# Sliding-window attention with a channel mix: batch 5's q and k through the DMA crossbar, batch 0's tail tokens in another row order

## The chip, the cores and the metric

The kernel runs on one core of one Trainium2 chip. The metric is the device time of one execution in microseconds (us), as the median of several runs. TensorE (PE) does matmuls and transposes, ScalarE (ACT) and VectorE (DVE) work on tiles elementwise, GpSimd (POOL) and SyncE (SP) issue most of the DMA transfers. Each engine executes its own list of instructions in order, and semaphores tie the lists together.

## The reference

Attention with a causal window of 128 tokens and a linear distance bias per head, followed by an RWKV channel mix over the concatenated heads:

```python
def _attn_ref(q, k, v):                 # [8 batches, 8 heads, 576 tokens, 64]
    ...
    scores = scale * np.matmul(q, k.transpose(0, 1, 3, 2))
    ...
    bias = slopes[:, None, None] * (-np.abs(rel).astype(np.float32))[None, :, :]
    mask = (rel >= 0) & (rel < window)
    ...
    return np.matmul(attn, v).astype(np.float32)      # attn: softmax of the masked scores

def _moe_ref(x, mu_k, mu_r, w_k, w_v, w_r):           # x: [8, 576, 512]
    ...
    xk = mu_k * x + (1.0 - mu_k) * x_prev             # x_prev: x one token earlier
    xr = mu_r * x + (1.0 - mu_r) * x_prev
    k = np.maximum(xk @ w_k, 0.0)                     # 512 to 1024
    v = k * k @ w_v                                   # 1024 to 512
    r = 1.0 / (1.0 + np.exp(-(xr @ w_r)))
    return (r * v).astype(np.float32)
```

Inputs and output are float32; the kernel computes in bf16 with float32 sums.

## The kernel before

**Tiles.** A batch has 576 tokens: four blocks of 128 and a tail of 64. Heads go in pairs (`g`, four of them), one head in each half of the 128 partitions. For each batch and pair the kernel brings q and k into a layout with the head dimension on partitions, computes scores (`scores`, matmuls on L727 into the PSUM tiles `duo`), takes exp on ACT (L741 into `at`), multiplies by a mask of bias and window on DVE (L754), and multiplies by v (`attend`, L782), where a column of ones gives the softmax sum. DVE divides (L788, L794 into `xu`), the result is transposed into `xt`, and DVE mixes it with its shifted self into `xk` and `xr` (L881, L888). The channel mix runs on pieces of 256 to 512 tokens out of two batches: L984 (w_k, then relu on ACT, L991, and a square on DVE or ACT into `kk`), L1002 (w_r, then tanh, L1009), L1018 (w_v) and L1023 on DVE into `ot`, which SP stores (L1048).

**Getting q and k transposed.** POOL loads a batch's q and k into one of two buffers `cb`, v into one of two `vs` and `tv`, and the tail tokens of q and k into one of two `ts`. There are two ways on. In batches 1 to 5, PE transposes blocks of `cb` by matmuls with the identity (`qk_quad` on L1079 for batches 1 and 2; `qk_some` on L838 for 3 to 5, half a batch at a time: 32 matmuls), and ACT or DVE copies the result from PSUM to one of four `qk` buffers (L697). For batches in `XB`, SP issues `dma_start_transpose` from `cb` (`flip`, L536): eight transfers per batch, one for each of q and k and each block of 128 tokens, into one of two buffers `qx`, which L727 reads directly. Each of them covers all heads, so the first score of a batch needs all eight. `full_load` reads rows in another order for batches in `XB` (`h (r p) d` instead of `h (p r) d`), with the same number of transfers. The two `qx` buffers also serve as staging space for batch 0 at the start.

**Tail tokens.** From batch 4 on, SP also transposes the tail tokens (`tail_flip`, L629) from `ts` to `tt`. Batches 1 to 3 do it on PE (L913). For batch 0 (`TW`), four tokens go into one row of 256 elements, so q and k make two loads of 128 rows (L516), and PE brings them into place with 16 matmuls on L940 against a permutation of the identity, from which DVE copies to `tt`.

**Order.** A planner at the top of the file (`Plan`) builds the program from nodes with costs. For PE, ACT and DVE the order of nodes is given by the lists in `ORDER` (node numbers, which change when nodes are added or dropped); SP and POOL issue in the order in which nodes were made, subject to when the planner thinks they are ready. 90 small matmuls on `warm` (L688) fill PE at the start. POOL's loads wait until the eighth load before them has landed.

## Time and profile before

| what | value |
|---|---|
| runs, median (lowest to highest) | 231.62 us (231.43 to 231.62), 3 runs |
| the profiled execution | 231.23 us, of which the span from first to last instruction is 229.5 us |
| granted TensorE clock | 1.0 throughout |
| DMA queue of POOL (software_dynamic) | 16.26 MB in 95,984 packets |
| DMA queue of SP and ACT (hardware_dynamic) | 13.84 MB in 23,776 packets |
| DMA transposes on SP | 16 `qx<-cb` (median 3.7 us to landing), 4 `tt<-ts` (4.5 us), 8 `xt<-xu` (2.5 us) |

Busy time counts the time in which an engine executes an instruction, over the span. PE matmuls overlap in its pipeline, so a merged row of the timeline is a little longer than the distance to the next one. The page also cuts the span into 40 slices of 5.7 us and gives the busy share of each in tenths:

```
PE   7999999999999999999999999999999999999994
ACT  3569999999899979999876757986448432435501
DMA  6999999999999999999695999996152133222005
```

PE is nearly full from the second slice on; the DMA engines are full for the first 18 slices and again around the loads of the last two batches.

### The profile page before, as it was taken

What the parts mean: (1) busy time and instruction counts of PE and PEld (TensorE: products, weight loads), DVE (VectorE), ACT (ScalarE), POOL (GpSimd) and SP (SyncE); (2) the same over time, 40 slices, a digit from 0 to 9 for tenths busy, and PEclk for the clock granted to TensorE, in tenths of its full rate; (3) what the DMA queues carried; (4) which work ended last, traced back from release to release, by engine and by line L of the source; (5) the groups of instructions that cost most, each with busy time, mean ns of one, the idle gap of its engine ahead of it and who ended that gap; (6) DMA issues with size and microseconds to landing.
All of it is one profiled execution on the core that took longest, in us unless ns stands there. A gap on an engine that the chain in (4) does not pass through costs nothing.

```text
span 229.5 us, 6623 instructions
## 1 busy us (share of the span) xinstructions
PE 220.9 (96%) x2681; PEld 134.4 (59%) x2715; DVE 189.5 (83%) x423; ACT 163.4 (71%) x295; POOL 92.6 (40%) x118
## 2 busy tenths in 40 slices
PE   7999999999999999999999999999999999999994
PEld 6576756755756656555655755545675445456542
DVE  6687799899869998988788998999979979774333
ACT  3569999999899979999876757986448432435501
POOL 8666655589878961982004970700000000000000
PEclk9999999999999999999999999999999999999999
DMA  6999999999999999999695999996152133222005
GB/s 159 177 175 190 191 161 200 190 185 158 200 130 191 163 117 184 112 144 151 139 162 90 165 167 136 107 137 198 47 95 71 46 133 73 65 93 91 3 14 214
DMA packets 121534, 31.11 MB, mean 136 GB/s; under 512 B 108184, under 2 KB 117664, under 8 KB 121504
## 3 DMA queue, kind: packets, MB, share of 16 engines
q0 software_dynamic: 95984, 16.26, 98.6%
q1 hardware_dynamic: 23776, 13.84, 25.4%
q10 hardware_dynamic: 1744, 0.59, 1.0%
q8 instruction: 21, 0.34, 0.6%
q14 instruction: 9, 0.07, 0.1%
HBM read 33.56 MB, written 9.44 MB: 187 GB/s over the span
## 4 chain that ended last, share of the span: by engine, by line
PE 74%; DMA 12%; DVE 5%; POOL 3%; issue 2%; ACT 2%; DVEq 0%; POOLq 0%; ACTq 0%
PE uno L1018 24%; PE uno L984 23%; PE uno L1002 12%; PE duo L782 7%; PE duo L727 5%; DMA wk_sb<-in_moe_w_k_dram 4%; DMA cb<-in_k_dram 4%; DMA wv_sb<-in_moe_w_v_dram 4%; PE uno L838 3%; ACT at L741 1%; DVE xk L888 1%; DVE at L754 1%; DVE ot L1023 1%; POOL vs L501 1%; POOL qx L497 1%
## 5 line engine op out<-in xcount | busy, mean ns | idle before, releaser
L984 PE MATMUL uno<-xk,wk_sb 128*128 128x256 bf16 (+2 forms) x412 | 71.9, 313 | 0.4
L741 ACT ACTIVATE at<-duo 128x1024 bf16<-128x1024 f32 (+2 forms) x68 | 65.2, 987 | 7.5 <-PE duo L727 7.3
L991 ACT ACTIVATE rl<-uno 128x256 bf16<-128x256 f32 (+2 forms) x104 | 47.3, 476 | 31.7 <-PE uno L984 23.7
L1018 PE MATMUL uno<-wv_sb,kk 128*128 128x512 bf16 (+2 forms) x277 | 67.3, 373 | 1.5 <-issue 0.6
L984 PEld LDWEIGHTS <-wk_sb 128*128 128x128 bf16 x416 | 38.6, 98 | 22.8 <-issue 0.7
L501 POOL DMA_DIRECT2D vs<-in_v_dram x32 | 28.4, 898 | 39.0 <-PE duo L782 33.5
L1018 PEld LDWEIGHTS <-kk 128*128 128x128 bf16 x296 | 27.1, 98 | 27.6 <-issue 0.5
L965 DVE TENSOR_TENSOR kk<-rl 128x256 bf16<-128x256 bf16 (+2 forms) x94 | 29.8, 339 | 13.5 <-ACT rl L991 13.3
L754 DVE TENSOR_TENSOR at<-at,mask 128x1024 bf16<-128x1024 bf16 x56 | 36.9, 686 | 2.4 <-ACT at L741 2.1
L1002 PE MATMUL uno<-wr_sb,xr 128*128 128x512 bf16 x133 | 35.6, 380 | 0.8 <-DMA wr_sb<-in_moe_w_r_dram 0.3
L1009 ACT ACTIVATE rs<-uno 128x512 bf16<-128x512 f32 x36 | 21.7, 614 | 17.0 <-PE uno L1002 11.4
L1023 DVE SCALAR_TENSOR_TENSOR ot<-rs,uno 128x512 f32<-128x512 bf16 (+2 forms) x37 | 24.2, 669 | 9.5 <-PE uno L1018 6.1
L888 DVE SCALAR_TENSOR_TENSOR xk<-dl,mu_sb,xt 128x576 bf16<-128x576 bf16 (+1 forms) x32 | 24.6, 778 | 0.2
L888 DVE SCALAR_TENSOR_TENSOR xr<-dl,mu_sb,xt 128x576 bf16<-128x576 bf16 (+1 forms) x32 | 24.7, 780 | 0.0
L782 PEld LDWEIGHTS <-at 128*128 128x128 bf16 x576 | 21.3, 98 | 4.8 <-issue 0.2
L794 DVE TENSOR_TENSOR xu<-duo,rc 128x640 bf16<-128x640 f32 x28 | 22.9, 822 | 0.5
L697 ACT COPY qk<-uno 128x512 bf16<-128x512 bf16 (+1 forms) x40 | 21.0, 586 | 1.2 <-PE uno L1127 0.9
L1002 PEld LDWEIGHTS <-xr 128*128 128x128 bf16 x144 | 13.3, 98 | 14.3 <-DMA wr_sb<-in_moe_w_r_dram 0.4
L532 POOL DMA_DIRECT2D cb<-in_k_dram x20 | 17.8, 917 | 3.8 <-DMA vs<-in_v_dram 1.9
L782 PE MATMUL duo<-vs,at 128*128 128x65 bf16 x448 | 18.8, 194 | 0.1
L532 POOL DMA_DIRECT2D cb<-in_q_dram x20 | 17.7, 923 | 2.2 <-PE uno L984 1.5
L697 ACT COPY xt<-uno 128x640 bf16<-128x640 bf16 (+3 forms) x28 | 15.1, 576 | 1.9 <-PE uno L838 0.9
(82 smaller groups left out, 200.5 us busy)
## 6 DMA issues: line engine op xcount, KB each, us to landing
out_dram<-ot SPq DMA_DIRECT2D x30, 256.0 KB, 3.9
vs<-in_v_dram POOLq DMA_DIRECT2D x32, 128.0 KB, 7.2
cb<-in_q_dram POOLq DMA_DIRECT2D x20, 128.0 KB, 6.3
cb<-in_k_dram POOLq DMA_DIRECT2D x20, 128.0 KB, 6.1
out_dram<-ot SPq DMA_DIRECT2D x10, 128.0 KB, 1.8
wk_sb<-in_moe_w_k_dram POOLq DMA_DIRECT2D x2, 512.0 KB, 8.8
cb<-in_q_dram POOLq DMA_DIRECT2D x4, 256.0 KB, 9.7
cb<-in_k_dram POOLq DMA_DIRECT2D x4, 256.0 KB, 10.0
```

The costliest lines, as they stand in the source:

```text
L501: return dma(POOL, 256, issue_t(1024), lambda e: nc.gpsimd.dma_start(out=vs_buf[h.idx][:, j, :, 0:D], in_=v[b, :, 128 * j:128 * j + 128].r ...
L532: return [dma(POOL, 256, issue_t(1024), lambda e, r=r: nc.gpsimd.dma_start(out=cb_buf[h.idx][:, i, r], in_=src[:, :, r]), [g], kind="q") f ...
L697: (nc.scalar.copy if e == ACT else nc.vector.tensor_copy)(out=out, in_=in_)
L741: lambda e, ah=ah, w=w, hp=hp: nc.scalar.activation(out=ah(), in_=two(hp)[:, :, 0:w], func=AF.Exp, scale=float(scale)), (), [hp])
L754: nc.vector.tensor_tensor(out=a, in0=a, in1=m, op=ALU.mult)
L782: nc.tensor.matmul(a[:, hl, t - t0], lhsT=at[:, lo:lo + 128], rhs=vs[:, u, 2 * g + hl, :] if u < NF else tvb[:, 2 * g + hl], start=(u == u ...
L888: lambda e: nc.vector.scalar_tensor_tensor(out=buf[hk.idx][:, g, e0 + c0:e0 + c1], in0=dls(), scalar=mu[:, g:g + 1], in1=xc(1), op0=ALU.mu ...
L965: nc.vector.tensor_tensor(out=out, in0=in_, in1=in_, op=ALU.mult)
L984: nc.tensor.matmul(one(hp)[:, 0:n], lhsT=wk_sb[:, po, 128 * fo:128 * fo + 128], rhs=xk_buf[hx.idx][:, po, c0:c1], start=(po == 0), stop=(p ...
L991: a = op(ACT, act_t(n), [s], pr, lambda e, hp=hp, hr=hr: nc.scalar.activation(out=rl_buf[hr.idx][:, 0:n], in_=one(hp)[:, 0:n], func=AF.Rel ...
L1002: nc.tensor.matmul(one(hp), lhsT=xr_buf[hx.idx][:, po, 128 * c:128 * c + 128], rhs=wr_sb[:, po], start=(po == 0), stop=(po == NPO - 1))
L1018: nc.tensor.matmul(one(hv)[:, a:b], lhsT=kk_buf[hk.idx][:, fo, o:o + 128], rhs=wv_sb[:, fo, a:b], start=(fo == 0), stop=(fo == NFO - 1))
```

## The change

Three edits and new lists. Batch 5 joins the batches whose q and k go through the DMA crossbar. In batch 0's tail load the 128 rows are ordered by token group first and head second (`c h`) instead of head first (`h c`), and the permutation in the L940 matmuls follows. The lists for PE, ACT and DVE are replaced; the numbers in them shift with the nodes that batch 5 drops and adds.

```diff
 ORDER = {
     "PE": [int(x) for x in """
-49 42 74 72 39 58 56 67 51 71 43 65 53 66 60 69 57 54 52 40 45 46 48 59 68 75 41 55 73 63 76 131 61 47 44 50 70
...
+42 76 47 65 59 73 39 58 48 50 71 68 63 74 75 41 43 55 46 61 40 66 51 52 45 56 57 67 70 53 69 131 60 44 49 72 144
...
-    XB = range(6, B)
+    XB = range(5, B)
     XO = range(6, B)
...
                     out=ts_buf[h.idx].rearrange("p h d -> p (h d)")[:, 256 * i:256 * i + 256],
-                    in_=(q, k)[i][b, :, SM:S].rearrange("h (c r) d -> h c (r d)", r=4)), [g], kind="ts"))
+                    in_=(q, k)[i][b, :, SM:S].rearrange("h (c r) d -> c h (r d)", r=4)), [g], kind="ts"))
...
                         lhsT=ts_buf[hs.idx][:, n],
-                        rhs=ident.rearrange("p (g t c) -> p t g c", g=G, t=2)[:, hl],
+                        rhs=ident.rearrange("p (c g t) -> p t g c", g=G, t=2)[:, hl],
                         start=True, stop=True)
```

On SP the order around batch 5 becomes (stores are numbered from the start of the program):

```
before: ... store 8, store 9, tail transpose b5, store 10, 2 x b6, store 11, 3 x b6, store 12, 2 x b6, store 13, 1 x b6, tail transpose b6, ...
after:  ... store 8, store 9, 8 x b5, tail transpose b5, store 10, store 11, store 12, 3 x b6, store 13, 5 x b6, store 14, tail transpose b6, store 15, store 16, 1 x b7, store 17, 7 x b7, ...
```

On PE 64 matmuls on L838 with their weight loads go. POOL's list is the same as before. The file is one line shorter, so line numbers behind the lists are lower by one.

## The prediction

> **What bounds the kernel now.** I read the page's busy line and chain first, then PE's waits cut to a window, then the chain's pieces up to 45 us, then the timelines of PE, POOL and SP around batch 5. The page:

> ```profile
> span 229.5 us, 6623 instructions
> PE 220.9 (96%) x2681; PEld 134.4 (59%) x2715; DVE 189.5 (83%) x423; ACT 163.4 (71%) x295; POOL 92.6 (40%) x118
> PEclk9999999999999999999999999999999999999999
> PE 74%; DMA 12%; DVE 5%; POOL 3%; issue 2%; ACT 2%; DVEq 0%; POOLq 0%; ACTq 0%
> ```

> TensorE is busy 96% at full granted clock, and the chain lies on it for 74%; the 12% on DMA need a place. PE's waits from 38 us to 226 us are two lines in all:

> ```profile
> PE uno L1018 <- issue: 0.6, 4, 0.2
> PE uno L1018 <- DVE at L754: 0.2, 1, 0.2
> ```

> So over 188 us PE stands for 0.8 us (total, count, longest). Work taken from PE there shortens the run one for one, and a late operand there lengthens it one for one; ACT and DVE work is hidden under PE. The chain's pieces show the DMA share:

> ```profile
> 5.73 9.91 DMA wk_sb<-in_moe_w_k_dram
> 17.42 9.35 DMA cb<-in_k_dram
> 28.20 9.28 DMA wv_sb<-in_moe_w_v_dram
> 37.52 1.02 PE uno L1018 x4
> ```

> Up to 37.5 us the chain is the stream of POOL loads: the first L1018 starts 0.04 us after its weights land. Before it PE idles 0.55 us for batch 1's tail tokens and 0.30 us for wr_sb (page lines for L913 and L1002 in its waits). That 0.85 us is what an earlier load stream can give back.

> **Part 1, batch 5's transposes leave PE.** The two bursts and what follows each:

> ```profile
> 102.97 0.63 PE L838 MATMUL uno<-ident,cb 64*128 64x64 bf16 x32
> 103.76 1.67 PE L1018 MATMUL uno<-wv_sb,kk 128*128 128x512 bf16 x7 [0.16 <-issue]
> 111.61 0.63 PE L838 MATMUL uno<-ident,cb 64*128 64x64 bf16 x32
> 112.17 1.04 PE L1018 MATMUL uno<-wv_sb,kk 128*128 128x512 bf16 x3
> ```

> The chain gives each burst of 32 matmuls 0.47 us (the 0.63 includes the drain of the last one), so 2 x 0.47 = 0.94 us go. All other PE instructions keep their number and size. The new order has 105 changes between 64-row and 128-row instructions, the old one 104; a change costs about 0.10 us (L727's last starts at 105.80, L984 at 105.92, where neighbours follow at 0.03). Net: **-0.84 us**, all in the stretch without waits.

> Off the path: of the 512-element qk copies ACT loses seven (603 ns each) and DVE one (687), and ACT takes four squares from DVE (two of 423, two of 515 ns). With one 256-element copy moved from DVE to ACT (409 against 376 ns) ACT loses 7 x 0.603 - 0.38 - 1.88 = 2.0 us and DVE 0.69 + 0.41 + 2 x 0.28 + 2 x 0.35 = 2.4 us. Costed at nothing, since PE hides both; neither gets heavier.

> Added: eight 128x512 crossbar transposes on SP, behind the ninth output store and ahead of batch 5's tail transpose and the tenth store. SP's rows:

> ```profile
> 84.50 2.99 SPq L1048 DMA_DIRECT2D out_dram<-ot  x2
> 92.38 1.22 SPq L629 DMA_TRANSPOSE tt<-ts  x1
> 105.55 0.34 SPq L1048 DMA_DIRECT2D out_dram<-ot  x1
> 105.98 3.04 SPq L536 DMA_TRANSPOSE qx<-cb  x2
> 139.59 11.94 SPq L536 DMA_TRANSPOSE qx<-cb  x8
> ```

> SP is free from 87.5 to 105.55 us but for one transpose. Batch 5's q and k land from 83.5 to 90.0 us (first issue 75.70 + 7.75, last 82.82 + 7.20). Eight issues take 10 to 12 us (1.23 us median; 11.94 for batch 7), so they run from 87.6 to about 99.6 us, the tail transpose to about 101 us, the tenth store is not delayed. The first score of batch 5 is at 111.2 us and needs all nine. How long they take to land beside loads is bounded by two rows: batch 6's eight, after the loads had ended, landed 2.5 to 4.0 us after issue; batch 7's, beside four loads of v, up to 8.0 us, 16.2 us from the first issue to the last landing (139.59 to 155.81). Batch 5's run beside cb of batch 6 and v of batch 5, so I take batch 7's row: last q/k landing 87.6 + 16.2 = 104 us, the tail transpose (6.55 us to land at 92.38) by 108 us. Slack 3 us and more: **0 us**. If that cover is gone it is rival 2.

> What they push back: eight transposes need some 8 us of the DMA engines (batch 7: 16.2 us minus four loads and tv at 0.83 us, over 12 us, is 1.0 us each), so v of batch 5 (landed by 101.3) may land by 109; batch 5's first L782 is at 129.7. Batch 6's load lands by 116 instead of 108; its transposes now stand behind the twelfth store (113.7) and a thirteenth, end near 125 instead of 119.2, and are read at 140.9. The fourteenth store waits 1.6 us longer for SP; five output buffers cover it. Batch 7 takes its qx buffer from batch 5, free after the last score at 126.2, first used at 139.6. Each has slack of 4 us or more: 0 us.

> [...]

> **Part 2, batch 0's tail tokens.** The two loads are issued at 6.47 and 7.09 us and land at 16.41 and 16.96, 0.77 and 0.55 us after the load before (wk_sb, 15.64). Batch 1's, the same bytes in 64-partition form, add 0.45 and 0.41 us (27.22 and 27.63 after 26.77). If the new row order brings them to the latter pace, the stream behind them gains 1.32 - 0.86 = 0.46 us. Bounds: nothing (the pace is not the order's), and half of it, 0.66. I take 0.46, the row of the same size. The sum feels it because chain and PE are load-bound at 37.5 us and 0.85 us of idle can be given back.

> [...]

> The new lists put one more memset ahead of `ident` on DVE (four of at_buf at 0.07 to 0.11 us each, one vs, instead of one at_buf, two vs, one xt): POOL's L448 waits for it, so all loads start about 0.1 us later: +0.1 us. The sixteen L940 matmuls read the identity at a stride of 8 elements instead of in runs of 16; no row shows that. They take 0.28 us now; between 0 and twice more (+0.56). I take 0: they stand at 17.25 us, ahead of the 0.55 us idle, which swallows it.

> **Sum.** -0.84 - 0.46 + 0.10 = -1.2 us. The profiled execution took 231.23 (span 229.5, 1.7 around it): 230.0. The median shown is 231.62, 0.39 above it: **230.4 us**.

> **Rivals.**
> 1. The tail load gives nothing (the stream's pace is set by other loads, or PE's 0.85 us turn up at another early wait). Then only part 1 counts: 231.62 - 0.84 = 230.8. For it: PE's early waits also hang on DVE (sid, id, 0.2 to 0.3 us each). Against it: the 0.04 us between wv_sb's landing and L1018.
> 2. Slower: batch 5's transposes land late and PE, in order, stands before its first score. If the loads went first, the transposes would end 8 x 1.3 = 10.4 us after 108.1, at 118.5 us: 7.3 us of stall less 1.2. It decides from 111.2 us on; the change loses when they land after 112.4. Between 112.4 and 118.5: 231.6 to 237.7, middle 234.6. For it: loads fill the DMA engines (9 tenths in these slices). Against it: batch 7's row, where both went on together.
> 3. The new lists bring small waits into the stretch that has none. The row for one is 0.2 us (L1018 on DVE at): six of them eat the gain, 231.6, no change. For it: all three lists are new. Against it: the order of PE differs from the old one by a few places, with ACT and DVE lighter.
> [...]

> **How the numbers follow.** Forecast 0.46, rival 1 0.20, rival 2 0.17, rival 3 0.16, rival 4 0.01. No change is within 0.2% (0.46 us, about what this kernel's runs tell apart), so faster is below 231.16. Forecast and rival 1 are faster but for a few hundredths each, rival 3 spreads around no change with some on the slower side, rivals 2 and 4 are slower: 0.63, 0.14, 0.23. The range takes the forecast with its ends (229.4 if the tail load gives 0.66 and small waits go as well, 231.0 with 0.56 for L940 and no catch-up), rivals 1 and 3, and the first part of rival 2: 229.3 to 232.4.

> **What would show it.** Right: no L838 on cb after batch 4, and PE's waits after 38 us still under 1 us; the first L1018 some 0.4 us earlier, with tail loads landing within 0.45 us of each other; eight transposes on SP between 87 and 101 us, the last landing before 111. Wrong: an idle PE before batch 5's first L727, released by DMA qx<-cb (rival 2); several short waits on ACT or DVE lines (rival 3); L1018 not earlier at 37.5 us (rival 1).

## The result and the profile after

The changed kernel took 233.62 us (median of 22 runs, 230.6 to 235.69), the kernel before 231.8 us beside it (22 runs, 231.19 to 234.13): a ratio of 1.0045, 95% interval 1.0023 to 1.0066. It is slower by 0.45%. The ratio leaves out seven of the changed kernel's 22 runs that took over 1.5% more than its fastest, five of them with a mean granted clock of 0.990 to 0.993; with them the medians lie 0.8% apart. The forecast was 230.4 us, the range ended at 232.4.

The profile that came with the result (`after` below) caught an execution with 3.4 us at half clock (told of at the end); the lines below come from a second profile of the same changed kernel (`r_after`), which ran at full clock throughout. Its lines are one lower than those of the kernel before (L727 is L726, L782 is L781, L1018 is L1017). The page:

```profile
span 231.1 us, 6540 instructions
PE 222.9 (96%) x2651; PEld 133.8 (58%) x2651; DVE 187.2 (81%) x417; ACT 160.9 (70%) x293; POOL 92.0 (40%) x118
PEclk9999999999999999999999999999999999999999
```

64 matmuls are gone from the program, but the span is 1.6 us longer than the 229.5 us before. PE's waits from 38 to 226 us (total, count, longest), where the kernel before had 0.8 us in all, none over 0.2 us:

```profile
PE duo L781 <- issue: 1.5, 1, 1.5
PE uno L983 <- ACT rl L990: 0.3, 1, 0.3
PE duo L726 <- DVE xu L793: 0.3, 1, 0.3
```

Three waits are new, and each has a place. The chain around 45 us (start, us, what):

```profile
44.16 0.38 PE uno L1078 x32
44.53 0.41 PE duo L781 x10
44.95 1.51 issue
46.45 0.40 PE duo L781 x8
```

PE stops in the middle of an attend, between two matmuls with the same operands, and nothing releases it. The second place is batch 6's division into `xu`. SP's transposes from `xu`, and DVE's rows (start, us, line):

```profile
167.42 6.08 SPq L902 DMA_TRANSPOSE xt<-xu  x4
```

```profile
166.53 1.56 DVE L793 TENSOR_TENSOR xu<-duo,rc 128x640 bf16<-128x640 f32 x2
168.63 0.82 DVE L793 TENSOR_TENSOR xu<-duo,rc 128x640 bf16<-128x640 f32 x1
171.45 0.82 DVE L793 TENSOR_TENSOR xu<-duo,rc 128x640 bf16<-128x640 f32 x1 [1.25 <-DMA xt<-xu]
```

There are three `xu` buffers. The fourth division needs the first buffer back, whose transpose was issued at 167.42 and landed at 171.35 us. In the kernel before, the fourth division waited for nothing:

```profile
164.83 0.82 DVE L794 TENSOR_TENSOR xu<-duo,rc 128x640 bf16<-128x640 f32 x1
169.56 0.82 DVE L794 TENSOR_TENSOR xu<-duo,rc 128x640 bf16<-128x640 f32 x1
```

There it began 4.73 us after the first. Here DVE was ready for it at 170.2 us, 3.7 us after the first: the new lists put the four divisions closer together. Until the fourth division has read its `duo`, PE cannot go on with the scores:

```profile
171.07 0.60 PE L983 MATMUL uno<-xk,wk_sb 128*128 128x256 bf16 x4
171.60 0.39 PE L726 MATMUL duo<-qx 64*128 64x256 bf16 x4
172.32 0.34 PE L726 MATMUL duo<-qx 64*128 64x256 bf16 x4 [0.33 <-DVE xu L793]
173.06 0.76 PE L983 MATMUL uno<-xk,wk_sb 128*128 128x256 bf16 x5 [0.34 <-ACT rl L990]
```

From one start to the next, the last L726 matmul ahead of each of the two waits takes 0.49 and 0.50 us longer than its columns, some 0.1 us of it for the shape change: 0.9 us lost. The second wait, on ACT, hangs on the first: neither is there in the profiles `a_xu4` and `a_shift40` (below), in which the fourth division does not wait.

A sum for this execution, from the starts of the same PE weight loads in both profiles (most of them, since the lists differ): 0.15 us late at 44 us, 1.9 at 52, 1.8 still at 96. Behind the two L838 bursts that are missing it is 0.85, so they gave 0.95. Behind the waits at 172 us it is 1.7 and stays so to the end, against +1.6 in the spans.

### The profile page after: what moved, and what is told of

Its sections match the earlier page's. It is cut to its first block, busy times and chain, and to the rows that moved or that the text cites. A ratio compares the mean times of both kernels' runs of the same rounds, so it can differ in the third digit from the quotient of the medians.

```text
span 233.3 us, 6540 instructions
## 1 busy us (share of the span) xinstructions
PE 225.4 (97%) x2651; PEld 135.2 (58%) x2651; DVE 187.1 (80%) x417; ACT 161.1 (69%) x293; POOL 92.1 (39%) x118
## 4 chain that ended last, share of the span: by engine, by line
PE 78%; DMA 14%; POOL 3%; issue 2%; DVE 1%; ACT 0%; DVEq 0%; POOLq 0%; SPq 0%; ACTq 0%
PE uno L1017 26%; PE uno L983 24%; PE uno L1001 13%; PE duo L781 6%; PE duo L726 6%; DMA wv_sb<-in_moe_w_v_dram 4%; DMA cb<-in_k_dram 4%; DMA wk_sb<-in_moe_w_k_dram 4%; PE uno L837 2%; DMA xt<-xu 2%; POOL vs L500 1%; PE uno L1078 1%; POOL qx L496 1%; POOL cb L496 1%; DVE xu L793 0%
## 5 line engine op out<-in xcount | busy, mean ns | idle before, releaser
L1017 PE MATMUL uno<-wv_sb,kk 128*128 128x512 bf16 (+2 forms) x296 | 69.2, 374 | 0.3 <-DMA wv_sb<-in_moe_w_v_dram 0.3
L1017 PEld LDWEIGHTS <-kk 128*128 128x128 bf16 x296 | 27.2, 98 | 29.2 <-DMA wv_sb<-in_moe_w_v_dram 0.6
L1001 PE MATMUL uno<-wr_sb,xr 128*128 128x512 bf16 x144 | 36.9, 383 | 0.0
L964 DVE TENSOR_TENSOR kk<-rl 128x256 bf16<-128x256 bf16 (+2 forms) x90 | 28.5, 337 | 10.2 <-ACT rl L990 10.0
L781 PEld LDWEIGHTS <-at 128*128 128x128 bf16 x576 | 21.0, 98 | 6.1 <-issue 2.0
L781 PE MATMUL duo<-vs,at 128*128 128x65 bf16 x448 | 18.8, 194 | 1.8 <-issue 1.8
L696 ACT COPY qk<-uno 128x512 bf16<-128x512 bf16 (+1 forms) x33 | 17.4, 588 | 1.7 <-PE uno L1126 1.0
L696 ACT COPY xt<-uno 128x512 bf16<-128x512 bf16 (+3 forms) x28 | 15.4, 589 | 3.5 <-PE uno L837 2.8
```

The costliest lines, as they stand in the source:

```text
L696: (nc.scalar.copy if e == ACT else nc.vector.tensor_copy)(out=out, in_=in_)
L781: nc.tensor.matmul(a[:, hl, t - t0], lhsT=at[:, lo:lo + 128], rhs=vs[:, u, 2 * g + hl, :] if u < NF else tvb[:, 2 * g + hl], start=(u == u ...
L964: nc.vector.tensor_tensor(out=out, in0=in_, in1=in_, op=ALU.mult)
L1001: nc.tensor.matmul(one(hp), lhsT=xr_buf[hx.idx][:, po, 128 * c:128 * c + 128], rhs=wr_sb[:, po], start=(po == 0), stop=(po == NPO - 1))
L1017: nc.tensor.matmul(one(hv)[:, a:b], lhsT=kk_buf[hk.idx][:, fo, o:o + 128], rhs=wv_sb[:, fo, a:b], start=(fo == 0), stop=(fo == NFO - 1))
```

## The experiments

Ratios are to the kernel before on the same chip, with 95% intervals. Points 1 and 3 ran on one chip, points 4, 5 and 6 on one other each, so ratios are compared across points only through the kernel before.

**1. The parts one by one.** `r_after` is the changed kernel again.

> The changed kernel once more, unchanged, for a second profile beside the first. In the first one PE lost 1.8 us at 44.9 us with no releaser shown, the granted clock dipped in the slice after it, and another 1.4 us went between 163 and 175 us, where DVE waited 1.8 us for an xu buffer (its transpose xt<-xu took 4.4 us to land). Theory L (the new lists are the cost): the wait on xt<-xu is there again and PE loses about 1 us between batch 6 and batch 7's second score; the stall at 45 us need not be. Theory F (the extra crossbar transposes are the cost): PE stands at batch 5's first score, or loads that follow the transposes are late. Theory N (disturbance of this execution): neither is there again and the time is 230 to 231 us.

`b_flip`: the old lists less the ten nodes that batch 5 drops (later node numbers lowered by 5 or 10), batch 5 through the crossbar, old tail load.

```diff
-    XB = range(6, B)
+    XB = range(5, B)
```

> Batch 5 through the crossbar with the OLD lists (the ten nodes of its PE transposes and copies struck out, the rest in the old order), and the old tail load. Theory L: 0.8 us faster than before (0.94 us of PE work less, no new waits): ratio 0.9965. Theory F: no faster, or slower by up to 1 us: ratio 1.000 to 1.005, as the whole change. Theory N: as theory L.

`b_tail`: the kernel before with the new order of the tail rows alone.

```diff
-... "h (c r) d -> h c (r d)" ...   "p (g t c) -> p t g c"
+... "h (c r) d -> c h (r d)" ...   "p (c g t) -> p t g c"
```

> Only the new row order of batch 0's tail load (and of the permutation in its 16 matmuls), old lists, no batch 5 in the crossbar. In the first profile of the changed kernel the two loads landed 0.49 and 0.48 us apart instead of 0.77 and 0.55, but the 16 matmuls took 0.9 us instead of 0.3 and the weights w_v landed at 37.61 us instead of 37.48. If the load's gain reaches the first L1018: 0.3 to 0.5 us faster, ratio 0.998. If the slower matmuls come through to the end: 0.3 to 0.6 us slower, ratio 1.002. If both are swallowed by the wait for w_v: 1.000.

`a_noflip`: the changed kernel with batch 5 back on PE, the ten nodes put into the new lists by hand.

```diff
-    XB = range(5, B)
+    XB = range(6, B)
```

> The NEW lists and the new tail load, but batch 5's transposes back on PE, put beside the same neighbours as in the old lists. Theory L: slower than before by the waits of the new lists, 1 to 2 us: ratio 1.005 to 1.009, with DVE xu waiting for xt<-xu again near 172 us. Theory F: as before, or 0.3 us faster by the tail load: ratio 0.998 to 1.001. Theory N: as theory F.

| kernel | ratio |
|---|---|
| r_after | 1.0039 (1.0003 to 1.0075) |
| b_flip | 0.9974 (0.9942 to 1.0005) |
| b_tail | 0.9996 (0.9964 to 1.0028) |
| a_noflip | 1.0264 (1.0215 to 1.0313) |

The crossbar with the old lists is not slower, the row order alone does nothing measurable, and the whole is slower: what is left is the new lists, or something that all of them share. By the ratios alone this is not settled, since the intervals of `b_flip` and `r_after` touch. `a_noflip` tells nothing of batch 5: put in by hand, the PSUM copies stand behind two exps on ACT, and PE waits for them (start, us, line):

```profile
115.75 0.63 PE L835 MATMUL uno<-ident,cb 64*128 64x64 bf16 x32
119.23 1.44 PE L981 MATMUL uno<-xk,wk_sb 128*128 128x384 bf16 x4 [2.85 <-ACT qk L694]
```

PE then runs at half clock for 6.8 us, and the ratio is far above the 1.005 to 1.009 expected. The kernel has the stop in the attend near 45 us too, of 1.4 us, and `b_flip` has two of 1.1 us elsewhere (lines of its PE waits):

```profile
PE duo L724 <- issue: 1.1, 1, 1.1
PE uno L1076 <- issue: 1.1, 1, 1.1
```

**2. What the stops have in common.** The page lists a DMA queue that no line of the kernel issues to:

```profile
q8 instruction: 20, 0.33, 0.6%
```

20 packets of 16 KB. PE's matmuls and weight loads are some 5,300 (2651 of each on the page), 265 to a packet; in the kernel before there are 21 packets for 5,396 of them, 257 to a packet. So these packets are taken for PE's program, and the stops below bear it out. Each recorded matmul was given a number (weight loads and matmuls count one each; the start of the count is the same for all, and only distances matter). The stops of over 0.9 us behind 8 us that nothing releases (start to start of the matmuls on either side), in the 20 profiles of this study:

```
profile          stops after   fetch began     PE reached the   PE went on, us
                 instruction   at us           number at us     after the fetch began
after            1451          44.0            44.7             2.7
r_after          1451          44.0            44.8             2.5
a_noflip         1451          44.0            44.8             2.5
a_xu4            1707          48.6            50.3             3.0
b_flip           429           15.3            17.2             3.1
b_flip           1707          49.4            50.8             2.8
bft_pid          429           15.1            16.6             2.8
bft_pid          1707          49.2            50.6             2.8
a_xu4_shift40    1197          34.1            35.7             2.6
a_xu4_shift40    1705          48.7            48.4             2.6
b_shift40        1707          47.5            47.6             2.5
bft_shift40      1197          33.5            34.6             3.4
bft_shift40_pid  1197          33.2            34.5             2.7
a_xu4_shift28    1707          48.8            50.0             2.6
bft_shift28_pid  1707          47.6            49.1             2.5
```

All 15 lie within two of 171 plus a multiple of 256 (427, 1195, 1451, 1707). PE goes on 2.5 to 3.4 us after the fetch began: the packet itself takes 1.0 to 2.0 us in the trace, and PE starts 1.3 to 2.0 us after its end. A stop is what is left of these when PE has arrived (in `after` 2.7 less 0.7, 2.0 us from start to start). In the kernel before the fetch for 1451 began at 41.8 us, 2.8 us ahead of PE: no stop. At the places of the stops PE had taken 3.4 to 5.7 us for the last 256 instructions, short transposes and attends standing close; behind 52 us it takes 6.3 us and more everywhere, and no stop lies there.

**3. Moving the numbers, and a fourth buffer.** In `a_shift28` and `a_shift40` 28 or 40 of the 90 warm-up matmuls are two of half the width: the same columns, 56 or 80 more instructions.

```diff
-        nc.tensor.matmul(one(h_wm)[:, 0:128], lhsT=warm, rhs=warm, start=True, stop=True)
+        for c in ((0, 64), (64, 128)) if i < 28 else ((0, 128),):
+            nc.tensor.matmul(one(h_wm)[:, c[0]:c[1]], lhsT=warm, rhs=warm[:, c[0]:c[1]], start=True, stop=True)
```

> The changed kernel with 28 of the 90 warm-up matmuls at the start split into two of half the width: 56 more instructions on PE, the same columns. Theory 1 (PE runs out of fetched instructions): in every profile with a stall that nothing releases, PE stops after instruction 171 + a multiple of 256 (1451 in three profiles of the new lists, at 44.7 us, 1.5 to 1.9 us; 429 and 1707 in one of the old lists), and the 16 KB fetch that ends the stall began only 0.7 to 1.9 us before. 56 more instructions ahead move these points to places that PE reaches at 49.7, 29.4 and 35.9 us, with 5.5, 6.3 and 6.5 us for the last 256 instructions instead of 5.5, 5.6 and 5.7. The stall of 1.5 us in the attend at 44.7 us is gone from the profile; if the fetches start no later than 3 us after they are due, no other takes its place, and the ratio falls by about 0.006, from 1.004 to 0.998. Theory 2 (the stall belongs to this attend: its operands or its PSUM): it stays at 44.7 us and the ratio stays at 1.004.

> The same with 40 warm-up matmuls split, 80 more instructions. Theory 1: one of the points now lies at 47.8 us, right behind the densest 256 instructions of the program, which PE executes in 3.7 us; a fetch that starts 2.6 to 5.0 us after it is due and takes 2.5 us until PE can go on leaves PE standing 1.4 to 3.8 us there. Nothing at 44.7 us. The ratio is 1.004 to 1.014, above that of 28 split. Theory 2: as the changed kernel, 1.004, the stall at 44.7 us.

```diff
-    NQ, NA, NX, NV, NC = 4, 4, 3, 2, 2
+    NQ, NA, NX, NV, NC = 4, 4, 4, 2, 2
```

> The changed kernel with four xu buffers instead of three. Theory 3 (the new lists bunch the four attends of batch 6, so the fourth xu needs the first buffer before its transpose has landed): DVE's wait of 1.25 us for xt<-xu at 171.5 us and the 1.0 us that PE loses in L726 at 171.7 to 173 us are gone, and the ratio falls by 0.004, to 1.000; the stall at 44.7 us stays. Rival (that wait was covered anyway): 1.004 as before.

`b_flip_tail` has `b_flip` and the new row order: both parts of the change in the old lists.

> The old lists, less the nodes that batch 5 drops, with both parts of the change: batch 5 through the crossbar and the new row order of the tail tokens. The lists alone are missing. If the new lists are the cost, this is faster than before: crossbar alone gave 0.9974, the row order alone 0.9996, so about 0.997; with the 0.46 us that the prediction gave to the row order 0.9955. If the two parts together are the cost (and not the lists), 1.004 as the changed kernel.

| kernel | ratio |
|---|---|
| a_shift28 | 1.0016 (0.9991 to 1.0042) |
| a_shift40 | 0.998 (0.9958 to 1.0002) |
| a_xu4 | 1.0005 (0.9981 to 1.003) |
| b_flip_tail | 1.0001 (0.9974 to 1.0029) |

The stop at 45 us is gone in both shifted kernels. One profile each proves little, since `a_xu4`, with nothing split, has no stop there either; with the table above it says that the stop belongs to the number and not to the attend. With 28 split the ratio is 1.0016, where 0.998 was expected, and the waits from 38 to 226 us are one line:

```profile
PE uno L984 <- ACT rl L991: 0.3, 1, 0.3
```

40 split was expected to be the worst and came out best of the two: the fetch for the dense place at 47.5 us began only 1.4 us after PE had passed the number 256 before it, where 2.6 to 5.0 were assumed. With four buffers DVE's wait and the 0.9 us in L726 are gone, and the ratio falls by 0.0034 where 0.004 was expected (the two intervals overlap). The same step in the shifted kernels (points 4 and 5) gives two answers: with 28 split 1.0016 falls to 0.9929, intervals apart; with 40 split 0.998 rises to 0.9993, inside the intervals, in profiles of which the first had no such wait and the second has two stops. In the execution of `a_xu4` PE stopped at 1707 instead of 1451:

```profile
PE duo L726 <- issue: 1.0, 1, 1.0
PE uno L1017 <- DMA wv_sb<-in_moe_w_v_dram: 0.4, 1, 0.4
```

How long the wait is hangs on the first transpose. Its time from issue to landing, and the wait of the fourth division, in profiles of the new lists:

```
profile     to landing, us   wait, us
after       4.44             1.76
r_after     3.94             1.25
a_shift28   3.48             0.79
a_shift40   2.40             0
a_noflip    2.40             0
a_xu4       4.30             0    (four buffers)
```

Three buffers leave it some 2.7 us, little more than the 2.4 us of the fastest transposes here. In `b_flip_tail`, with the old lists, it is issued at 164.37, lands at 166.77, and is needed at 168.22: 3.8 us. That is not always enough either: in `bft_shift40_pid` below, with the old lists, the transpose takes 4.06 us and the fourth division waits 0.22.

The profile of `b_flip_tail` is one without a stop, of the fastest of its 12 runs, and there the prediction's sum is nearly all found (page, and PE's row of the first w_v matmuls: start, us, line):

```profile
span 228.1 us, 6547 instructions
PE 223.2 (98%) x2651; PEld 134.6 (59%) x2651; DVE 189.0 (83%) x423; ACT 159.5 (70%) x287; POOL 92.2 (40%) x118
```

```profile
36.90 1.02 PE L1015 MATMUL uno<-wv_sb,kk 128*128 128x512 bf16 x4
```

The span is 1.4 us below the 229.5 before: 0.6 us at the first w_v matmul (36.90 against 37.52), still 0.6 at 94 us, and 0.7 more behind 112 us, where batch 5's bursts are missing. The 0.6 at the start is a draw, as the spread of the first w_v matmul will show (under the tail load, below). Yet over 12 runs, with spans from 228.1 to 231.3 us, the ratio is 1.0001.

**4. Both remedies, and the control.** `a_xu4_shift40` has four buffers and 40 split, `b_shift40` is the kernel before with 40 split, `bft_shift40` is `b_flip_tail` with 40 split, and `bft_shift40_pid` has besides the permuted identity of the tail's 16 matmuls copied into a tile of its own:

```diff
+    pid = cst.tile([128, 2, G, 128 // (2 * G)], BF16, name="pid")
...
+        nc.vector.tensor_copy(out=pid, in_=ident.rearrange("p (c g t) -> p t g c", g=G, t=2))
...
-                        rhs=ident.rearrange("p (c g t) -> p t g c", g=G, t=2)[:, hl],
+                        rhs=pid[:, hl],
```

> The changed kernel with both remedies: four xu buffers and 40 split warm-up matmuls. If the xu wait (0.0034 of the time) and the dry points of PE's instruction stream (0.006) are two separate losses, they add: 1.004 - 0.009 = 0.995, and the profile shows neither a wait of DVE for xt<-xu near 170 us nor a stop of over 1 us that nothing releases. If the lists cost by many small waits, or if 40 split was only a lucky draw, 0.998 to 1.000.

> The kernel before with 40 split warm-up matmuls: the control. Its stretch from 38 to 52 us has the same 256-instruction windows as the changed kernel (5.7 and 5.4 us at instructions 1451 and 1707), so if dry points cost it something in some of its runs, it gains too: 0.996 to 0.998. If they are a loss of the new lists alone: 1.000.

> The old lists less the dropped nodes, both parts of the change, 40 split. Dry points as a general loss: 1.0001 falls to 0.994 to 0.996 (its fastest run, 228.1 us of span, is 1.1 us below the fastest of the kernel before, 229.2). If the split does nothing here: 1.000.

> The same, with the permuted identity of the tail's 16 matmuls copied once into a tile of its own, so that they read it in one run of 64 elements. If the stride of 8 elements is what made them take 1.03 us instead of 0.37, they are back at 0.37 us, and what follows at 18 us comes 0.66 us earlier. If the idle time for batch 1's tail tokens swallows that, the ratio stays that of the kernel without the copy; if not, it is 0.001 to 0.003 lower.

| kernel | ratio |
|---|---|
| a_xu4_shift40 | 0.9993 (0.9965 to 1.0021) |
| b_shift40 | 1.0015 (0.9988 to 1.0042) |
| bft_shift40 | 0.9987 (0.9963 to 1.0011) |
| bft_shift40_pid | 0.9979 (0.9951 to 1.0006) |

All four miss what was hoped for, and all four profiles have stops, 1.0 to 2.8 us (the table above): 40 is a bad place after all, as first expected. The one good result, 0.998 for `a_shift40`, may be a draw: its interval overlaps those of the four. The kernel before stops there too, so the stops are no property of the new lists. `b_shift40`'s PE rows:

```profile
47.16 0.82 PE L1003 MATMUL uno<-wr_sb,xr 128*128 128x512 bf16 x2
49.97 0.57 PE L1003 MATMUL uno<-wr_sb,xr 128*128 128x512 bf16 x1 [2.00 <-issue]
```

**5. The better place.** By the time that PE takes for 256 instructions in the profiles of the changed kernel, 28 split leaves one number with 5.5 us and the others with 6.3 and more.

> The changed kernel with four xu buffers and 28 split warm-up matmuls (points at 49.7, 29.4 and 35.9 us with 5.5, 6.3 and 6.5 us for 256 instructions). Theory 1: 1.0016 (28 split, three buffers) less 0.0034 is 0.998; 0.995 if the stops are gone entirely. Rival (the split does nothing): 1.0005, as with four buffers alone.

> The kernel before with 28 split: the control. If its own median carries stops of this kind (its runs spread over 229.2 to 231.8 us of span), 0.996 to 0.998. If not, 1.000.

> Old lists, both parts of the change, the permuted identity in a tile of its own, nothing split. Its points lie where the kernel before has them, with the same time for the last 256 instructions. If the stops strike it as often as the kernel before, the whole gain of the parts shows: 0.995. If they strike more often (as the measured 1.0001 without the tile says): 0.998 to 1.000.

> The same with 28 split. Theory 1: 0.993 to 0.996, the lowest of all. Rival: as without the split.

| kernel | ratio |
|---|---|
| a_xu4_shift28 | 0.9929 (0.9901 to 0.9957) |
| b_shift28 | 0.9981 (0.9958 to 1.0004) |
| bft_pid | 0.9997 (0.9969 to 1.0024) |
| bft_shift28_pid | 0.9957 (0.9935 to 0.9979) |

The changed kernel with both remedies beats the kernel before by 0.7%, more than the 0.2 to 0.5% expected, and the control with the same shift by 0.0052, 1.2 us (each of the two ratios is known to some 0.6 us). The four buffers alone gave 1.0005, so the shift is worth 0.0076 in that kernel, with intervals that do not meet. In the old lists it is worth 0.0040 (`bft_pid` to `bft_shift28_pid`, intervals that just overlap), 0.0019 in the kernel before, where no change is still inside the interval. Even so two of the three shifted profiles of this table have a stop at 1707 (1.4 and 1.0 us), and the three others with 28 split in this study have none: the shift does not end the stops, and whether it makes them shorter or rarer is argued from the ratios.

**6. What the tail's part is worth there.** `a_xu4_shift28_pid` adds the tile; `a_xu4_shift28_oldtail` takes the old row order instead.

> The changed kernel with four xu buffers, 28 split, and the permuted identity in a tile of its own. The 0.66 us that the 16 matmuls lose at 17 us lie ahead of PE's idle time for batch 1's tail tokens at 27 us (0.5 us in the kernel without the tile), so most of it is swallowed: 0.9925 to 0.993, no change that can be measured. If it is not swallowed: 0.990.

> The changed kernel with four xu buffers and 28 split, the tail tokens of batch 0 loaded in the old row order (and their matmuls on the identity in the old order). If the new row order is worth the 0.46 us of the prediction: 0.995. If it is worth nothing, as the row order alone (0.9996) said: 0.993.

They came to 0.994 (0.9916 to 0.9964) and 0.9956 (0.9928 to 0.9984). Neither differs from 0.9929 by more than the intervals; the row order's worth, between nothing and some 0.6 us, stays open. The 16 matmuls are back at their old pace with the tile (L939 in the changed kernel, L945 with the tile):

```profile
17.57 1.10 PE L939 MATMUL uno<-ident,ts 128*64 128x64 bf16 x16
```

```profile
17.63 0.44 PE L945 MATMUL uno<-pid,ts 128*64 128x64 bf16 x16
```

The waits from 38 to 226 us of `a_xu4_shift28_pid`, where nothing is left but four gaps of 0.2 us at L1023 (the L1018 of the kernel before):

```profile
PE uno L1023 <- issue: 0.6, 4, 0.2
```

## Why the prediction was wrong

**The step that failed** is the sentence that the two bursts' time falls out "all in the stretch without waits", and with it the reason given against rival 3: "the order of PE differs from the old one by a few places, with ACT and DVE lighter". The new lists were costed at one shape change. In that stretch the second profile loses 1.7 us at 45 us and 0.9 at 172. The second loss comes with the new lists: a wait on DMA xt<-xu at 171.5 us. With a fourth buffer it is gone, in a profile whose transpose lands as late (4.30 us). The trace shows that; the ratios leave its worth open, falling by 0.0034 and 0.0087 in two pairs and rising by 0.0013 in the third. In the PE list 306 of 423 nodes stand in another place, half of all within two places and one as far as 57 away, and on ACT and DVE the farthest moved by 21 and 30. Rival 3 was right in kind and wrong in size: not six waits of 0.2 us, but two of 0.3 with one cause, 0.9 us in all, and their place, a chain from PE over DVE and SP back to a buffer, was not looked for, since the kernel before had no wait in it. The risk stood in the rows, though: three buffers, four divisions, and a transpose that takes 2.4 us and more. How long it takes changes from one execution to the next, and with it the wait: 4.44 and 3.94 us in the two profiles of the changed kernel, with waits of 1.76 and 1.25.

**What the sum had no term for** is the instruction stream, the 1.7 us of the first loss. Against the forecast of -1.2 us the second profile stands at +1.7, 2.9 us apart: 1.7 for this stop, 0.9 for the `xu` wait, 0.5 for the start up to 44 us (forecast -0.36, found +0.15), less 0.1 for the bursts. Dropping 64 matmuls with their weight loads does not move the numbers before 52 us, but what shifts PE against the fetches by a microsecond or two can decide whether one is late: the one for 1451 began 2.8 us ahead of PE in the kernel before, 0.7 and 0.8 in `after` and `r_after`. Shown: where the stops lie, that they follow the number and not the operation, and that moving the numbers by 56 in the changed kernel with four buffers takes the ratio from 1.0005 to 0.9929 (by 80 it stays at 0.9993). Not shown: why, before 52 us, a fetch began anything from 1 to 6 us after PE had passed the number 256 before (the page has the DMA engines at nine tenths then, but in the changed kernel it has them so up to 121 us, and fetches begin up to 4.0 us behind that number later too, where PE is slower); and whether the new lists make the stop at 1451 likelier. Three of their four profiles without a shift have it, none of five of the old lists has, but two of those stop at 1707.

**Point by point.**

- Batch 5's bursts, -0.84: right in size. 0.70 us between `b_flip_tail` and the kernel before in the stretch behind 94 us, 0.95 in the second profile of the changed kernel. All parts together gave 0.0052 of 231.6, or 1.2 us, in the shifted kernels; that this is the forecast's sum is in part luck, since the tail's share in it is not shown.
- Late transposes (rival 2): did not come. In `r_after`, SP's rows are

```profile
88.88 12.20 SPq L535 DMA_TRANSPOSE qx<-cb  x8
101.25 1.19 SPq L628 DMA_TRANSPOSE tt<-ts  x1
106.69 5.43 SPq L1047 DMA_DIRECT2D out_dram<-ot  x3
```

  The eight issues take 12.2 us (10 to 12 were taken), the last lands at 108.84 (104), the tail's at 109.90 (108), and the first score, itself 2 us late, is at 113.34: 3.4 us of slack. Batch 7's row was the right one to cost them by. v of batch 5 landed by 105.4 (109 taken), batch 6's load by 116.9 (116).
- Rival 4, at 0.01: no run shows a time for a single 128x128 block in the crossbar. What `r_after` shows is that the eight transposes, 32 such blocks, were through in 20 us (88.88 to 108.84), beside loads and stores.
- The tail load, -0.46: mis-sized. From wk_sb's landing to the second tail load's took 1.32 us in the profile before and 1.03 to 1.34 in the four others with the old order (middle of the five 1.07); with the new one the middle of 15 profiles is 0.94 (0.79 to 1.66). The profile before, from which the 0.46 was taken, was among the slowest of its kind. And the first w_v matmul is no earlier for it that could be told: 36.90 to 39.04 us with the new order (middle 37.77), 37.30 to 38.55 with the old one (middle 37.89). The gain of 0.1 to 0.4 us at 16 us drowns in what else moves the first 37 us from one profile to the next, by a microsecond and more; rival 1 is not excluded. No run shows the 0.66 us that the forecast's lower end of 229.4 was worked out with: against the 1.32 of the profile before, the fastest of the 15 gained 0.53.
- The memset, +0.10: did not come. POOL's first load of q is issued at 4.00 us before and 3.99 after.
- The strided identity, taken as 0 between bounds of 0 and 0.56: mis-sized. From its start to the next instruction it takes 1.03 us instead of 0.37, +0.66. The cover named for it held: `bft_shift40_pid` is 0.7 us ahead of `bft_shift40` at instruction 683 (21.6 against 22.3 us) and level at 939 (28.7 in both).

## What to carry to other kernels

When PE has no wait, look for the buffer rings that are just long enough (count producers, consumers and the landing of a transpose between them), because a new order finds the one that is one short. Where many short matmuls stand together while DMA is full, number PE's instructions and see how long it takes for each 256 ahead of the stops (here 3.4 to 5.7 us, and 6.3 and more behind 52 us, where no stop lies): an idle time "issue" in the middle of a group of like matmuls is the mark, and some more or fewer warm-up instructions can move it (here 56 or 80). A change of half a per cent is judged by a control that has the same alignment, not by the kernel before alone.

## What the hardware showed unexpectedly

Half clock (granted 0.50) followed some of the stops. In the profile that came with the result PE stopped for 1.8 us at 44.9 us and the clock was at half from 47.9 us for 3.41 us; in `b_shift40` (stop from 47.6, 2.0 us) from 50.05 to 53.47. The windows of `b_shift40` (stretch, its length, busy us and instructions of PE, PEld, DVE, ACT and POOL, PEclk, the DMA packets' time over that of 16 engines, GB/s):

```profile
44.00:47.00 3.00, 3.00 (x120) 2.58 (x108) 2.79 (x7) 2.97 (x7) 1.56 (x2) 1.00 2.05 207
50.10:53.40 3.30, 3.30 (x33) 1.69 (x34) 2.33 (x4) 1.25 (x4) 2.90 (x4) 0.50 2.28 162
```

Stops of 1.5 us in the second profile of the changed kernel and 2.1 us in `bft_shift40` had no such sequel. In these profiles it goes with where a stop falls. All clock changes of a profile lie whole steps of 3.413 us apart: `after` has 40.96 us at full clock (12 steps), 3.41 at half and 180.9 at full (53), the kernel before 225.28 at full (66). Cut into these steps up to the last matmul, the 20 profiles have four steps at full clock in which PE stood for 1.77 to 2.44 us, over half of the step, and half clock followed each; in all others PE stood for at most 1.56 us, and full clock went on. The 2.1 us of `bft_shift40` fall into two steps, 1.32 and 0.85 us. Half clock lasted 3.41 us in three profiles and 6.83 in `a_noflip`; in the steps ahead of it PE stood for 52 to 71% of the time.

A moving operand with a stride of 8 bf16 elements (16 bytes) makes 16 matmuls of 64 columns take 1.03 us instead of 0.37. With the same elements in one run, in a tile of their own, they are back at 0.37 (`a_xu4_shift28_pid`, 17.63 to 18.00 us).
